# A linear-attention and feed-forward kernel: batch 0's stages in a new order, norms' small values in PSUM, batch 1's attention out in plain float32, dummy matmuls in PE's waits

## The chip, the cores and the metric

One Trainium2 chip, and of it one core. The metric is the device time of one execution in microseconds (us), lower is better. "Time" without more is the median over several runs; a profile shows one execution. The engines are PE (matrix multiplies), DVE (vector), ACT (scalar functions), POOL (GpSimd) and SP, which here only issues DMAs.

## The reference

Linear attention without a softmax over 8 batches of 8 heads (576 tokens, 64 values per head), an RMS norm of each head's output, and a feed-forward block with SiLU over the 4608 tokens:

```python
kv = np.einsum('bhsd,bhse->bhde', k, v)
out = np.einsum('bhsd,bhde->bhse', q, kv)
rms = np.sqrt(np.mean(out * out, axis=-1, keepdims=True) + 1e-06)
x = (out / rms * g_norm)          # transposed to 4608 tokens x 512
h = x @ w_in                      # 512 -> 2048
g = h * (1.0 / (1.0 + np.exp(-h)))
return g @ w_out                  # 2048 -> 512
```

## The kernel before

**Feed-forward.** The 4608 tokens are 9 tiles (t) of 512. Each tile takes 16 steps (f), one for each 128 of the 2048 inner values. A step makes `products` (h of the step: 12 matmuls of 128x512, from the four 128-rows c of x), `gate` (SiLU on ACT twice, and their difference), and `project` of the step two before (12 matmuls into four banks `acc`, one per 128 tokens). There are 144 steps, and PE is given their matmuls in the order of the code.

**Split operands.** A float32 value is kept as two float32r parts, a high one and the rest: `xh` and `xl` for x, `gh` and `gl` for the gate, `w[:, 0]` and `w[:, 1]` for weights. A product takes three matmuls: high by rest, rest by high, high by high. Weights arrive as 64-bit words and are converted block by block, wi0 to wi15 and wo0 to wo15, all during tile 0: `magnitude` (ACT `Abs`, then a clamp on POOL), `bits` (three DVE operations that build the float32 number, through a PSUM tile `conv`), `split_block` (ACT casts the high part, POOL subtracts it for the rest). Step f of tile 0 works on the bits of block wi f+2 and wo f, and splits those of the step before.

**Attention.** A batch is 4 pairs of heads. `mm_kv` makes a pair's two 64x64 kv (20 instructions on PE), ACT copies them to `kvm`, `mm_out` multiplies q by it in two halves of 288 tokens, ACT squares and copies, DVE sums the squares (`sum_sq`). When all 4 pairs are summed, `rsqrt` turns 72 sums per partition into inverse roots by a bit trick and three Newton steps on DVE; before that it adds the two heads' sums across partitions, with four copies of 32 partitions (L397). `spread`, `scale` and `to_tile` then write x. For batches 1 to 7 all of this stands among the feed-forward steps of the tile before: `plan(b, g)` puts each stage into `first_jobs`, `mid_jobs`, `last_jobs` or `chains` of a step, where `mid` stands between products and project. q, kv and kvm are split there (`qh`, `ql`, `kh`, `kl`).

**The start.** Batch 0 has no feed-forward work to stand among. `FirstPair` does its first 512 tokens in plain float32, with tokens on partitions: `make_kv`, `copy_kv`, `make_out` (four matmuls), `square` (ACT), `norm` (`token_norm`: reduce, add eps, inverse root on ACT, one Newton step, multiply to `on`), `make_x` (four transposes on PE), `to_tile`. `Rest` does the last 64 tokens of all four pairs. wi0, wi1 and wi2 are converted in between, the products of steps 0 and 1 are made one c at a time as x comes (`warm`), and `keep_warm` runs matmuls of the identity whose result nobody reads, six at the very start.

What sets the order: every engine runs its instructions in the order of the code, and waits only for the semaphores of what it reads or overwrites. DMAs go through SP's queue, in the order of the list `ORDER` (p is a pair of batch 0, b one of batch 1, g is g_norm).

Of the kernel before, what the change touches and what calls it, by code (L numbers as in the profile page):

```python
# [24 lines left out]
    wi0 p0 g p1 p2 wi1 p3 wi2 wo0 wi3 wo1 wi4 wo2 b0 wi5 wo3 b1 wi6 wo4 wi7 wo5 b2  # L25
# [5 lines left out]
def linear_attention_rms_silu_ffn(  # L31
# [48 lines left out]
    gcol = const.tile([P, 1], F32, name="gcol")  # L80

# [25 lines left out]
    def magnitude(kind, f):  # L107

        full = full_tile(kind, f)
        nc.scalar.activation(out=full, in_=low_high(kind, f)[1].bitcast(F32), func=AF.Abs)  # L110
        nc.gpsimd.tensor_scalar(  # L111
            out=full, in0=full, scalar1=LARGEST, scalar2=SMALLEST, op0=ALU.min, op1=ALU.max
        )

    def bits(kind, f):
# [3 lines left out]

        low, high = low_high(kind, f)  # L120
        first = []
        full = fulls.get((kind, f))
        early = full is None
        if early:
            full = full_tile(kind, f)
            first = [
                lambda: nc.vector.tensor_scalar(
                    out=b, in0=high, scalar1=0x7FFFFFFF, scalar2=None, op0=ALU.bitwise_and
                ),
                lambda: nc.vector.tensor_scalar(  # L130
                    out=full, in0=full, scalar1=SMALLEST, scalar2=LARGEST, op0=ALU.max, op1=ALU.min
                ),
            ]
        b = full.bitcast(I32)
        mids = [b] if early else []
# [6 lines left out]
        return first + [  # L142
# [44 lines left out]
    def newton(y, u, m):  # L187
        return [
            lambda: nc.vector.scalar_tensor_tensor(out=u, in0=y, scalar=-0.5, in1=y, op0=ALU.mult, op1=ALU.mult),
            lambda: nc.vector.tensor_tensor(out=u, in0=u, in1=m, op=ALU.mult),  # L190
            lambda: nc.vector.scalar_tensor_tensor(out=y, in0=u, scalar=1.5, in1=y, op0=ALU.add, op1=ALU.mult),
        ]

    class Pair:


        def __init__(self, b, c):
            self.b, self.c = b, c
            self.kvm = kvm[c if b == 0 else c % 2]
# [11 lines left out]
        def mm_kv(self, kv=None):  # L211
            kv = at_bank() if kv is None else kv
            self.kv = [kv[h * D:(h + 1) * D, 0:D] for h in range(2)]
# [12 lines left out]
        def split_kv(self):  # L226
            self.copy_kv()
            self.kh = kvp.tile([P, P], F32R, name="kh")
# [4 lines left out]
        def split_q(self):  # L233
            self.qh = tmp.tile([P, S], F32R, name="qh", tag="tmp")
# [8 lines left out]
        def mm_out(self, half):  # L243

            self.w = w = slice(half * HS, (half + 1) * HS)
            self.ps = ps = at_bank()[:, :HS]
            nc.tensor.matmul(out=ps, lhsT=self.kh, rhs=self.ql[:, w], start=True, stop=False)  # L247
# [39 lines left out]
    class FirstPair(Pair):  # L287
# [4 lines left out]
        def __init__(self, c):  # L292
            super().__init__(0, c)
            self.ps = at_bank("other") if c == 0 else None

        def make_kv(self):
            self.mm_kv(h_bank())

        def make_out(self):
            self.ps = self.ps or acc_bank()  # L300
# [8 lines left out]
        def norm(self):  # L309
            self.o = tmp.tile([P, S], F32, name="on", tag="tmp")[:, :512]  # L310
            return token_norm(self.o, self.ps, self.sq)
# [12 lines left out]
    class Rest:  # L324
# [13 lines left out]
        def norm(self):  # L338
            self.on = tmp.tile([P, S], F32, name="on", tag="tmp")[:, :256]
            return token_norm(self.on, self.o, self.sq)  # L340
# [16 lines left out]
    def token_norm(o, ps, sq):  # L357

        n = o.shape[1] // D
        m, u, y = (small.tile([P, 8], F32, name=name)[:, :n] for name in ("m0", "u0", "y0"))  # L360
        by_head = [t.rearrange("p (j d) -> p j d", d=D) for t in (o, ps, sq)]
        return [
            lambda: nc.vector.tensor_reduce(out=m, in_=by_head[2], axis=AX.X, op=ALU.add),
            lambda: nc.vector.tensor_scalar(
                out=m, in0=m, scalar1=1.0, scalar2=D * EPS, op0=ALU.mult, op1=ALU.add
            ),
            lambda: nc.scalar.activation(out=y, in_=m, func=AF.Abs_reciprocal_sqrt),
        ] + newton(y, u, m) + [
# [136 lines left out]
    with tc.manual_schedule():  # L505
# [78 lines left out]
        for f in range(WARM):  # L584
            products(warm[f], 0, f, 2)
# [96 lines left out]
```

## Time and profile before

| | |
|---|---|
| median of 3 runs | 897.2 us (897.12 to 897.44) |
| the profiled execution | 895.82 us, of which span 894.0 us |
| mean granted PE clock | 0.988 |
| PE busy | 869.1 us (97%) |
| DVE, ACT, POOL busy | 320.1, 302.7, 175.8 us |
| PE busy from 0 to 36 us | 26.56 us |
| PE busy from 36 to 46 us | 5.00 us |
| PE busy from 46 to 136 us | 82.63 us |

How to read it: the span is the time from the first to the last instruction of one execution, and the rest of its time lies around it. PE's busy time counts a matmul as long as its record says, so a matmul at half the clock counts twice as much. Steps of tile 0 can be told in the timeline by the `products` of line 428 with the tile `hp`: those of step 2 begin at 41.82 us, those of step 15 at 130.49 us.

### The profile page before, as it was taken

The numbers are of one execution on the slowest core, as the hardware profiler recorded it, in microseconds if no ns is written. First come the engines' busy times: TensorE is split into PE (matmuls) and PEld (weight loads), VectorE is DVE, ScalarE is ACT, GpSimd is POOL, SyncE is SP. The second block draws the span as 40 slices with busy tenths as digits, with TensorE's granted clock in tenths as the row PEclk, the third lists the DMA queues.
The fourth block names the chain that finished last, engine by engine and source line by source line (L and its number), as shares of the span: only waits on it lengthen the run. The fifth ranks groups of instructions, "written<-read, shape, count | busy, mean of one in ns | idle before, by whom it ended". The sixth has DMA issues, their size and how long they took to land.

```text
span 894.0 us, 10971 instructions
## 1 busy us (share of the span) xinstructions
PE 869.1 (97%) x4382; PEld 712.4 (80%) x4382; DVE 320.1 (36%) x588; ACT 302.7 (34%) x675; POOL 175.8 (20%) x172
## 2 busy tenths in 40 slices
PE   7689989999999999999999999999999999999998
PEld 5468868888888888888888888888888888888887
DVE  3788894224132423232333223231523141111111
ACT  3457734332243224322433234322432231112112
POOL 1388964101121002101210112010210020000000
PEclk9799999999999999999999999999999999999999
DMA  9538302310042003200311013100300010001001
GB/s 334 233 135 338 111 1 75 93 40 0 1 138 69 1 1 127 80 1 0 114 54 40 1 63 105 41 1 1 127 1 0 1 48 1 0 1 48 1 1 47
DMA packets 23971, 55.23 MB, mean 62 GB/s; under 512 B 2800, under 2 KB 3056, under 8 KB 23920
## 3 DMA queue, kind: packets, MB, share of 16 engines
q1 hardware_dynamic: 23920, 54.54, 17.7%
q8 instruction: 34, 0.56, 0.3%
q14 instruction: 17, 0.14, 0.0%
HBM read 45.09 MB, written 9.44 MB: 61 GB/s over the span
## 4 chain that ended last, share of the span: by engine, by line
PE 86%; DVE 5%; POOL 4%; issue 2%; ACT 1%; DMA 1%; SPq 0%; DVEq 0%; POOLq 0%; ACTq 0%
PE hp L428 40%; PE acc L458 40%; PE at L217 2%; POOL wi L158 1%; POOL full L111 1%; POOL gl L439 1%; PE at L248 1%; PE at L249 1%; PE at L247 1%; PE at L458 1%; DVE m L397 1%; DVE full L149 1%; DMA early_wi<-in_v 1%; PE hp L217 1%; DVE full L130 0%
## 5 line engine op out<-in xcount | busy, mean ns | idle before, releaser
L428 PE MATMUL hp<-xh,wi 128*128 128x512 f32 x1144 | 356.4, 393 | 1.9 <-POOL wi L158 1.9
L458 PE MATMUL acc<-wo,gh 128*128 128x512 f32 (+1 forms) x1152 | 355.2, 390 | 0.0
L439 DVE TENSOR_TENSOR gl<-gf,gh 128x512 fp32r<-128x512 f32 x128 | 88.7, 693 | 499.8 <-ACT gf L438 499.8
L428 PEld LDWEIGHTS hp<-xh,wi 128*128 128x128 f32 x1144 | 217.0, 190 | 45.8 <-POOL wi L158 2.5
L458 PEld LDWEIGHTS acc<-wo,gh 128*128 128x128 f32 x1152 | 214.9, 188 | 44.0
L428 PE MATMUL hp<-xl,wi 128*128 128x512 f32 x572 | 228.5, 400 | 3.5 <-ACT wi L157 3.5
L437 ACT ACTIVATE gh<-hp 128x512 fp32r<-128x512 f32 x143 | 85.5, 598 | 416.6 <-PE hp L428 416.4
L458 PE MATMUL acc<-wo,gl 128*128 128x512 f32 x576 | 222.5, 386 | 0.0
L428 PEld LDWEIGHTS hp<-xl,wi 128*128 128x128 f32 x572 | 108.5, 190 | 26.7 <-ACT wi L157 3.9
L458 PEld LDWEIGHTS acc<-wo,gl 128*128 128x128 f32 x576 | 108.2, 188 | 23.8
L283 POOL TENSOR_TENSOR xl<-o,xh 128x448 fp32r<-128x448 f32 (+7 forms) x56 | 53.2, 952 | 343.4 <-ACT xh L282 343.4
L438 ACT ACTIVATE gf<-hp 128x512 f32<-128x512 f32 x143 | 84.7, 592 | 0.0
L237 POOL TENSOR_TENSOR ql<-q,qh 128x576 fp32r<-128x576 f32 x28 | 40.1, 1432 | 176.3 <-ACT qh L236 172.2
L253 ACT ACTIVATE sq<-at 128x288 f32<-128x288 f32 x56 | 23.2, 414 | 39.6 <-PE at L249 39.6
L274 DVE SCALAR_TENSOR_TENSOR o<-o,gcol,yT 128x448 f32<-128x448 f32 (+7 forms) x56 | 33.8, 604 | 2.0
L224 ACT COPY kvm<-at 64x64 f32<-64x64 f32 x56 | 11.6, 207 | 58.5 <-PE at L217 58.2
L217 PEld LDWEIGHTS at<-v,k 128*64 128x64 f32 (+1 forms) x560 | 20.8, 136 | 13.3 <-issue 9.7
L217 PE MATMUL at<-v,k 128*64 128x64 f32 (+1 forms) x560 | 26.5, 231 | 1.2 <-ACT o L254 1.2
L282 ACT CAST xh<-o 128x448 fp32r<-128x448 f32 (+7 forms) x56 | 24.8, 442 | 5.0 <-DVE o L274 5.0
L267 DVE STREAM_TRANSPOSE yT<-y 128x448 f32<-128x448 f32 (+7 forms) x56 | 26.4, 471 | 0.0
L158 POOL TENSOR_TENSOR wi<-full,wi 128x512 fp32r<-128x512 f32 x16 | 20.8, 1301 | 20.3 <-ACT wi L157 20.3
L254 ACT COPY o<-at 128x288 f32<-128x288 f32 x56 | 22.7, 406 | 4.2 <-POOL xl L283 4.2
(98 smaller groups left out, 481.0 us busy)
## 6 DMA issues: line engine op xcount, KB each, us to landing
out<-ob SPq DMA_DIRECT2D x35, 256.0 KB, 2.3
wi<-in_moe_w_in SPq DMA_DIRECT2D x16, 512.0 KB, 8.1
wo<-in_moe_w_out SPq DMA_DIRECT2D x16, 512.0 KB, 9.2
k<-in_k SPq DMA_DIRECT2D x28, 288.0 KB, 2.9
v<-in_v SPq DMA_DIRECT2D x28, 288.0 KB, 3.2
q<-in_q SPq DMA_DIRECT2D x28, 288.0 KB, 2.9
early_wo<-in_k SPq DMA_DIRECT2D x2, 288.0 KB, 4.8
early_wi<-in_v SPq DMA_DIRECT2D x2, 288.0 KB, 5.1
```

The lines of the kernel that those rows point to most:

```text
L158: nc.gpsimd.tensor_tensor(out=w[:, 1, :], in0=full, in1=w[:, 0, :].bitcast(F32), op=ALU.subtract)
L217: nc.tensor.matmul(out=self.kv[h], lhsT=self.k[rows, c, :], rhs=self.v[rows, c, :], start=(r == 0), stop=(r == 4))
L237: nc.gpsimd.tensor_tensor(out=self.ql, in0=self.q, in1=self.qh.bitcast(F32), op=ALU.subtract)
L267: nc.vector.transpose(out=self.yT.rearrange("p (j a) -> p j a", a=32), in_=y[:, a // 32:e // 32].unsqueeze(2).to_broadcast([P, (e - a) // ...
L274: nc.vector.scalar_tensor_tensor(out=self.o[:, a:e], in0=self.o[:, a:e], scalar=gcol, in1=self.yT, op0=ALU.mult, op1=ALU.mult)
L282: nc.scalar.copy(out=th[:, self.c, w], in_=self.o[:, a:e])
L283: nc.gpsimd.tensor_tensor(out=tl[:, self.c, w], in0=self.o[:, a:e], in1=th[:, self.c, w].bitcast(F32), op=ALU.subtract)
L428: nc.tensor.matmul(out=hp[:, :TN], lhsT=w[:, a, fs], rhs=x[:, c, :], start=(c == 0 and i == 0), stop=(c == NP - 1 and i == 2),)
L437: nc.scalar.activation(out=gh, in_=hp[:, :TN], func=AF.Silu)
L438: nc.scalar.activation(out=gf, in_=hp[:, :TN], func=AF.Silu)
L439: (nc.gpsimd if t == 0 else nc.vector).tensor_tensor(out=gl, in0=gf, in1=gh.bitcast(F32), op=ALU.subtract)
L458: nc.tensor.matmul(out=bank, lhsT=g[:, ns], rhs=w[:, a, cs], start=(f == 0 and i == 0), stop=(f == NF - 1 and i == 2))
```

## The change

- **Order of the start.** Loads: pair 0's k, v and q now come before wi0, and wi1 before pairs 1 to 3. The stages of the four pairs, the conversions of wi0, wi1, wi2 and wo0 and the products of steps 0 and 1 are written out one call after another in a new order; the conversions go through `magnitude` and `conv`, and x of pairs 0, 2 and 3 (before: 2 and 3) is made the shorter way (`fast`). The products of step 2 now precede the transposes of `Rest`.
- **Dummies.** 41 identity matmuls in place of 6, at 10 places of the start.
- **Small values in PSUM.** `token_norm` keeps its sums and intermediate values in a PSUM bank (`stats`), and eps goes into the bias of the activation and into the Newton step. In `rsqrt` two float32 matmuls (L408, L409: `ones` by a row of D*EPS, and `both`, which adds partition blocks of 32 in twos, by the sums) put m into PSUM, in place of four copies and an addition; this holds for all batches from 1 on.
- **Batch 1.** `plain = b < 2`: q, kv and kvm are not split, and a half of out is one float32 matmul. Its stages stand closer together (`stage`, by thirds of a step), begin at step 3 instead of 2, and its `rsqrt` stands in step 11 instead of 12.

```diff
-    wi0 p0 g p1 p2 wi1 p3 wi2 wo0 wi3 wo1 wi4 wo2 b0 wi5 wo3 b1 wi6 wo4 wi7 wo5 b2
+    p0 wi0 g wi1 p1 p2 p3 wi2 wo0 wi3 wo1 wi4 wo2 b0 wi5 wo3 b1 wi6 wo4 wi7 wo5 b2
...
+    both = const.tile([P, P], F32, name="both")
+    nc.gpsimd.tensor_copy(out=both, in_=ident)
+    for i in range(4):
+        nc.gpsimd.tensor_copy(
+            out=both[32 * i:32 * i + 32, 32 * (i ^ 1):32 * (i ^ 1) + 32], in_=ident[32 * i:32 * i + 32, 32 * i:32 * i + 32]
+        )
+    ones = const.tile([1, 2 * P], F32, name="ones")
...
-    def newton(y, u, m):
+    def newton(y, u, m, eps=0.0):
+
         return [
-            lambda: nc.vector.scalar_tensor_tensor(out=u, in0=y, scalar=-0.5, in1=y, op0=ALU.mult, op1=ALU.mult),
-            lambda: nc.vector.tensor_tensor(out=u, in0=u, in1=m, op=ALU.mult),
+            lambda: nc.vector.scalar_tensor_tensor(out=u, in0=m, scalar=eps, in1=y, op0=ALU.add, op1=ALU.mult),
+            lambda: nc.vector.scalar_tensor_tensor(out=u, in0=u, scalar=-0.5, in1=y, op0=ALU.mult, op1=ALU.mult),
...
+            self.plain = b < 2
...
+            if self.plain:
+                nc.tensor.matmul(out=ps, lhsT=self.kvm, rhs=self.q[:, w], start=True, stop=True)
+                return
             nc.tensor.matmul(out=ps, lhsT=self.kh, rhs=self.ql[:, w], start=True, stop=False)
...
-        m, u = (small.tile(sums.shape, F32, name=name) for name in ("m", "u"))
-        calls = [
-            lambda i=i: nc.vector.tensor_copy(
-                out=m[32 * i:32 * i + 32], in_=sums[32 * (i ^ 1):32 * (i ^ 1) + 32]
-            )
-            for i in range(4)
-        ]
...
+        n = NP * (S // 32)
+        bank = at_bank()
+        m, u = bank[:, 0:n], bank[:, n:2 * n]
+        sums, y = (t.rearrange("p c j -> p (c j)") for t in (sums, y))
+        nc.tensor.matmul(out=m, lhsT=ones[:, :P], rhs=ones[:, P:P + n], start=True, stop=False)
+        nc.tensor.matmul(out=m, lhsT=both, rhs=sums, start=False, stop=True)
...
+            if b == 1:
+                k = 3 * g + 1 + 4 * p.c
+                stage(k, p.mm_kv)
+                stage(k + 1, p.split_kv)
+                stage(k + 2, p.begin_out, half[0])
+                stage(k + 3, half[1])
+                stage(k + 5, *[begin] * (p.c == 0), sums)
+                continue
...
-        second = plan(1, 2)
+        second = plan(1, 3)
...
-        keep_warm(6)
...
+        keep_warm(10)
         p0.make_kv()
+        keep_warm(2)
         p0.copy_kv()
+        magnitude("wi", 0, True)
+        w("wi0", 1)
+        p0.make_out()
+        keep_warm(8)
...
-        at(last_jobs, 1, rest.make_x, lambda: moves.extend(rest.to_tile()), lambda: moves.pop(0)())
+        at(mid_jobs, 2, rest.make_x, lambda: moves.extend(rest.to_tile()), lambda: moves.pop(0)())
```

What the new order comes to, engine by engine (numbers behind a name tell one buffer from another; `early_wi` and `early_wo` are batch 0's k, v and q, which lie in places of later weights).

PE, the start, before: dummies, then the pairs' kv (L217), out (L303) and transposes (L316).

```order
L526 MATMUL hp<-ident 128x128 x6
L217 MATMUL hp<-early_wi_114,early_wo_113 64x64 x10
L303 MATMUL at<-kvm_91,early_wo_115 128x128 x4
L217 MATMUL hp<-early_wo_122,early_wi_121 64x64 x10
L303 MATMUL acc<-kvm_92,early_wi_123 128x128 x4
L217 MATMUL hp<-early_wi_128,early_wo_127 64x64 x10
L316 MATMUL at<-ident,on 128x128 x4
L303 MATMUL acc<-kvm_93,early_wo_129 128x128 x4
```

PE, the same place after (L222 is kv, L314 out, L327 a transpose, L542 a dummy):

```order
L542 MATMUL hp<-ident 128x128 x10
L222 MATMUL hp<-early_wi_122,early_wo_121 64x64 x10
L542 MATMUL hp<-ident 128x128 x2
L314 MATMUL acc<-kvm_91,early_wo_123 128x128 x4
L542 MATMUL hp<-ident 128x128 x8
L222 MATMUL hp<-early_wo_134,early_wi_133 64x64 x10
L542 MATMUL hp<-ident 128x128 x2
L327 MATMUL acc<-ident,on 128x128 x4
L314 MATMUL acc<-kvm_92,early_wi_135 128x128 x4
L542 MATMUL hp<-ident 128x128
L222 MATMUL hp<-early_wi_140,early_wo_139 64x64 x10
```

The real work keeps its order but for pair 0's transposes, which now come ahead of pair 1's out, and dummies fill the places between.

DVE, tile 0, before: the chain of batch 1's norms in step 12, one for one among the conversions of wi14 (213) and wo12 (215); the names `m`, `u`, `y` are in SBUF, `conv` is in PSUM.

```order
L143 TENSOR_SCALAR conv<-full 128x512
L397 COPY m<-sums 32x72
L146 SCALAR_TENSOR_TENSOR conv<-wi_213,conv 128x512
L397 COPY m<-sums 32x72
L149 SCALAR_TENSOR_TENSOR full<-wi_213,conv 128x512
L397 COPY m<-sums 32x72
L143 TENSOR_SCALAR conv<-full 128x512
L397 COPY m<-sums 32x72
L146 SCALAR_TENSOR_TENSOR conv<-wo_215,conv 128x512
L402 SCALAR_TENSOR_TENSOR m<-m,sums 128x72
```

DVE, after, in step 11, among the conversions of wi13 (219) and wo11 (221); `at` is the PSUM bank with m and u:

```order
L146 TENSOR_SCALAR conv<-full 128x512
L410 TENSOR_SCALAR y<-at 128x72
L149 SCALAR_TENSOR_TENSOR conv<-wi_219,conv 128x512
L193 SCALAR_TENSOR_TENSOR at<-at,y 128x72
L152 SCALAR_TENSOR_TENSOR full<-wi_219,conv 128x512
L194 SCALAR_TENSOR_TENSOR at<-at,y 128x72
L146 TENSOR_SCALAR conv<-full 128x512
L195 SCALAR_TENSOR_TENSOR y<-at,y 128x72
```

The copies and the addition are gone, the chain has ten operations instead of fifteen, and it starts a step earlier.

PE, the end of the start, before: last products of steps 0 and 1, transposes of `Rest` (L345), products of step 2 (wi_425).

```order
L428 MATMUL acc<-xl_311,wi_380 128x512
L428 MATMUL acc<-xh_310,wi_380 128x512 x2
L345 MATMUL at<-ident,on 128x128 x2
L428 MATMUL hp<-xl_311,wi_425 128x512
L428 MATMUL hp<-xh_310,wi_425 128x512 x2
```

PE, the same place after (wi_460 is step 2's block, L356 the transposes of `Rest`, L462 the first project):

```order
L432 MATMUL acc<-xl_318,wi_432 128x512
L432 MATMUL acc<-xh_317,wi_432 128x512 x2
L432 MATMUL hp<-xl_318,wi_460 128x512
L432 MATMUL hp<-xh_317,wi_460 128x512 x2
L356 MATMUL at<-ident,on 128x128 x2
L462 MATMUL acc<-wo_488,gh 128x512 x2
```

All twelve products of step 2 (two rows of them are shown) now stand ahead of the transposes of `Rest`.

More of the change, by code (lines that the diff above doesn't have):

```diff
@@ L581, in linear_attention_rms_silu_ffn @@
[L581 to L582 removed]
+        n(p2, 4)
+        x(p1, 2)
+        magnitude("wi", 2)
+        n(p3, 2)
+        p2.make_x()
+        warm_products(0, 0)
+        keep_warm(6, kv_bank)
+        w("wi1", 1)
+        n(p3, 4)
+        split("wi", 1)
+        x(p2, 2, True)
+        w("wi2", 1)
+        p3.make_x()
+        magnitude("wo", 0)
+        warm_products(1, 0)
+        keep_warm(1, kv_bank)
+        x(p3, 2, True)
+        warm_products(0, 1)
+        warm_products(1, 1)
@@ L583, in linear_attention_rms_silu_ffn @@
+        w("wi2", 2)
         split("wi", 2)
-        for f in range(WARM):
-            products(warm[f], 0, f, 2)
+        warm_products(2, 0, 1)
+        rest = Rest()
         rest.make_out()
         rest.square()
+        magnitude("wi", 3)
+        w("wo0", 1)
         rest_norm = rest.norm()
-        wo0 = bits("wo", 0)
-        run(wo0[:3])
-        run(rest_norm[:3])
+        run(rest_norm[:2])
+        w("wo0", 2)
         table(AF.Silu)
-        run(wo0[3:])
         split("wo", 0)
-        at(chains, 0, lambda: rest_norm[3:])
+        run(rest_norm[2:])
```

185 lines of the change are left out of this document (99 added, 86 removed).

## The prediction

> **What bounds the kernel now.** I read the page's engine lines and slices first:
>
> ```profile
> span 894.0 us, 10971 instructions
> PE 869.1 (97%) x4382; PEld 712.4 (80%) x4382; DVE 320.1 (36%) x588; ACT 302.7 (34%) x675; POOL 175.8 (20%) x172
> PEclk9799999999999999999999999999999999999999
> ```
>
> PE has work in 97% of the span. So a faster helper engine is worth nothing by itself; the change can only take out time in which PE waits, or runs at half clock, and pays for each matmul it adds. Busy time by stretches says where those are (columns: stretch, its length, busy PE, PEld, DVE, ACT, POOL, granted clock, DMA):
>
> ```profile
> 16.40:19.80 3.40, 1.65 (x14) 1.29 (x14) 0.94 (x2) 1.84 (x6) 1.26 (x1) 0.99 1.02 405
> 19.80:30.00 10.20, 7.79 (x42) 6.38 (x43) 7.50 (x16) 4.21 (x9) 2.54 (x2) 0.50 1.04 402
> 36.50:41.50 5.00, 0.01 (x1) 0.02 (x1) 4.69 (x12) 3.07 (x7) 1.38 (x2) 0.87 0.00 0
> 41.50:47.00 5.50, 5.49 (x14) 4.44 (x15) 5.36 (x6) 3.79 (x8) 5.50 (x5) 0.50 0.00 1
> 47.00:126.80 79.80, 76.76 (x405) 61.88 (x403) 68.35 (x101) 49.19 (x105) 66.13 (x65) 1.00 0.44 164
> 126.80:131.90 5.10, 0.77 (x3) 0.24 (x2) 4.82 (x8) 1.44 (x3) 3.96 (x3) 1.00 0.02 3
> 131.90:136.00 4.10, 4.10 (x11) 3.23 (x12) 4.00 (x7) 3.19 (x6) 3.23 (x3) 0.58 0.00 2
> 136.00:801.00 665.00, 665.00 (x3341) 545.00 (x3341) 200.42 (x397) 211.25 (x488) 89.22 (x82) 1.00 0.13 41
> ```
>
> From 136 us on PE never stops, so everything is decided before. There are two places: the first 47 us (batch 0's stages, 5 us without PE at 36.5, half clock twice), and 126.8 to 136. PE's waits name them:
>
> ```profile
> PE at L345 <- DVE on L369: 5.0, 1, 5.0
> PE acc L303 <- ACT kvm L224: 4.1, 3, 1.8
> PE hp L428 <- ACT wi L157: 3.5, 1, 3.5
> ```
>
> **Term A, the start up to step 2's products.** Before, these start at 41.82. Durations, from the timeline and the chain (start, length, ...) and from the groups by form of 0 to 46 us (mean ns before the bar's idle part):
>
> ```profile
> 1.92 2.93 PE L526 MATMUL hp<-ident 128*128 128x128 f32 x12 [1.92 <-POOL ident masks.py:199]
> 14.65 1.53 PE L217 MATMUL hp<-early_wi,early_wo 128*64 128x64 f32 x20
> 16.11 0.72 PE L316 MATMUL at<-ident,on 128*128 128x128 f32 x4
> 18.59 1.16 PE L303 MATMUL acc<-kvm,early_wo 128*128 128x128 f32 x8 [1.75 <-ACT kvm L224]
> 24.05 2.08 PE L303 MATMUL acc<-kvm,early_wi 128*128 128x128 f32 x8 [1.80 <-ACT kvm L224]
> 41.82 0.78 PE L428 MATMUL hp<-xl,wi 128*128 128x512 f32 x1
> 49.91 0.95 PE L217 MATMUL at<-v,k 128*64 128x64 f32 x20
> 158.20 2.94 PE hp L428 x12
> L307 ACT ACTIVATE sq<-acc 128x512 f32<-128x512 f32 x3 | 1.8, 597 | 3.8 <-PE acc L303 3.8
> L224 ACT COPY kvm<-hp 64x64 f32<-64x64 f32 x8 | 1.6, 206 | 6.8 <-PE hp L217 6.8
> L363 DVE TENSOR_REDUCE m<-sq 128x8 f32<-128x512 f32 x4 | 2.7, 682 | 5.3 <-ACT sq L307 5.3
> L369 DVE TENSOR_TENSOR on<-acc,y 128x512 f32<-128x512 f32 x3 | 2.1, 692 | 0.3
> L146 DVE SCALAR_TENSOR_TENSOR full<-wo,full 128x512 int32<-128x512 int32 x1 | 0.7, 685 | 0.0
> L367 ACT ACTIVATE y<-m 128x8 f32<-128x8 f32 x4 | 0.8, 209 | 2.7 <-DVE m L364 2.7
> L191 DVE SCALAR_TENSOR_TENSOR y<-u,y 128x8 f32<-128x8 f32 x4 | 0.7, 166 | 0.1
> ```
>
> The clock doubles every PE price: kv 1.53 against 0.95, out 2.08 against 1.16. (Until 16 us the clock column reads full, but the 1.53 at 14.65 is a half-clock length: here the lengths are to be trusted.) A dummy costs 2.93/6 = 0.49 at half clock, 0.25 at full. In the new order PE begins at 2.0, as before, with ten dummies: to 6.9. If they bring the full clock, pair 0's kv ends at 7.9, its copies (2 x 0.21) at 8.4, out at 9.6, square 10.3, reduce 11.0, the weight operation put between 11.7, three small operations 12.3, on 13.0. PE meanwhile does eight dummies (2.0), pair 1's kv and two dummies: 13.05. From there PE's own list is the longest: three out (3.5), two kv (1.9), four times four transposes (2.9), 19 dummies (4.8), 24 products (5.9, twice the row of 12), the rest's out (0.5, an estimate: fewer columns than half an out): 19.5, so step 2 starts at 32.5. I went through ACT and DVE pair by pair with the same rows: on 3 is there at 25.2 for a transpose at 25.6, and the last x some 2 us before its use. The loads: pair 0's now come ahead of wi0, so earlier than before; wi1 (512 KB) now passes p1 and p2 on SP's queue, 1.3 us at the 400 GB/s of the rows above, which kv 1 at 11.6 leaves room for within 0.3. POOL's copies for `both` lie before its first subtraction. The m + eps operation goes into ACT's bias, one of 0.17 less per pair. **A = 32.5 - 41.8 = -9.3.** Bounds: 2 us earlier, 3.5 later (0.05 to 0.1 more at each of some 35 hand-overs, a clock that comes one stretch of 3.4 us late).
>
> **Term B.** Step 2's products take 47.0 - 41.8 = 5.2 at half clock, 2.9 at full: **-2.3**, with the rest's transposes now behind them.
>
> **Term C, stalls from 47 to 126.8:** 79.80 - 76.76 = 3.0 before. New ones come at step 2: after it ACT still has the table load, wo0's upper half, one magnitude and two SiLUs, and POOL gl, so the third project matmul waits some 1.8, and step 3's low half (POOL, after two gl) 1.3. POOL does five such things per step (two splits, two magnitudes, gl), and ql is gone for batch 1 (so are qh and kh on ACT and kl on DVE, which lay beside PE and count as nothing):
>
> ```profile
> 46.00:136.00 90.00, 74.31 (x72) 0.98 0.39 145
> L237 POOL TENSOR_TENSOR ql<-q,qh 128x576 fp32r<-128x576 f32 x4 | 5.8, 1456 | 4.2 <-ACT qh L236 4.2
> ```
>
> That leaves 68.5 us of POOL work for a stretch of some 84, 82% as before: PE stays the bound. **C = +0.3**, bounds -3 (nothing waits) and +4 (each step of a conversion late once). SP's loads of b2 and b3 wait for kv and now for out in place of POOL's ql; those come 9 us earlier too.
>
> **Term D, the end of tile 0.** The chain of batch 1's norms stands among the conversions of wi14 and wo12 on DVE:
>
> ```profile
> 110.82 1.30 POOL L158 TENSOR_TENSOR wi<-full,wi 128x512 fp32r<-128x512 f32 x1
> 111.03 3.54 DVE L397 COPY m<-sums 32x72 f32<-32x72 f32 x1
> 112.07 1.30 POOL L158 TENSOR_TENSOR wo<-full,wo 128x512 fp32r<-128x512 f32 x1
> 113.33 1.20 POOL L111 TENSOR_SCALAR full<-full 128x512 f32<-128x512 f32 x2
> 116.63 0.19 DVE L397 COPY m<-sums 32x72 f32<-32x72 f32 x1
> 130.49 0.50 PE L428 MATMUL hp<-xl,wi 128*128 128x512 f32 x1 [3.48 <-ACT wi L157]
> ```
>
> The same copy of 72 elements takes 0.19, or 3.54 for as long as POOL is busy from 110.82 to 114.53. DVE falls behind, wi15 is converted last, PE waits 5.10 - 0.77 = 4.3 and then runs 4.1 us at 0.58, of which 1.6 are lost. After, the four copies and the sum are two matmuls, the ten operations left have at most one SBUF input, and the chain stands a step earlier: 10 x 0.25 + 6 x 0.69 = 6.6 us of DVE in that step, then 1.35 + 4.1 in the next two, against 5.5 of PE: 1 us behind, with a step's slack. **D = -5.9**, bounds 0 and -5.9.
>
> **Terms E and F, work added on PE.** Batch 1's out: three matmuls of 0.13 per half before; plain float32 has no row of 288 columns. Out at full clock spaces its 8 instructions by (1.16 - 0.29)/7 = 0.124 per 128 columns, so 0.56 for 288: +0.17 eight times, **E = +1.3** (to 2.1 if 1.16 is scaled whole). The sums' two matmuls of 72 columns are four such instructions, 0.28 to 0.5 us; I take 0.35, nearer to scaling by columns, in seven batches: **F = +2.4**. All of it is on PE's path; after 136 us it is the only term.
>
> Sum: -9.3 - 2.3 + 0.3 - 5.9 + 1.3 + 2.4 = **-13.5**. The profiled execution took 895.8 (span 894.0 and 1.8 around it), so 882.3; the median of the runs, 897.2, lies 1.4 above it: **883.7**.
>
> **A rule against it.** The row of 16.4 to 19.8 has PE busy 1.65 of 3.4, longest gap 1.75, and 10.2 us at half clock follow. C's two gaps lie in one such stretch, and a stretch of dense PE at half clock costs 1.6 (D's row). The Trainium skill, TensorE: Matmul & The Clock Gate, "Why this matters for your kernels", wants no gap over about 3 us and would charge nothing for these; by its rule the sum stays -13.5, by the row it is -11.9. I go by the sum without it and keep 1.6 in the range. The page's "free-running" window of 3.4 us also means that the first full clock can come later in one execution than in another, which this one trace cannot show.
>
> **Rivals.**
> 1. Slower: the dummies don't bring the full clock, and stand ahead of the real work. Then PE's whole start, some 25 us at full clock (10.3 of it 41 dummies), takes 50: step 2 at 52.3, A = +10.5, B = 0, and the sum +8.6: 905.8. It decides once some 14 us of those 25 run at half clock. Against it: between 13 and 16.4 PE worked without a gap, and the 0.72 and 1.16 rows followed at full clock. 4%.
> 2. POOL sets tile 0's pace, or DVE's small operations stay slow in PSUM (the change doesn't do what it says there): the end of tile 0 still stalls, D = 0, 889.6. For it: POOL is busy 82%; against: conversions with one PSUM operand keep 0.69 beside POOL. 13%.
> 3. The start is bound by ACT, DVE and loads, so full clock buys half of it: A + B = -7, 888.3. 10%.
> 4. All stalls go, C = -3, A two better: 878.4. 8%.
>
> **How the numbers follow.** My forecast (881 to 887 with its own bounds) has 65%. 0.2% (1.8 us) is about what a measurement of this kernel can tell. The range 877.5 to 890.5 holds rivals 2 to 4 and leaves out rival 1 and some 15% of tails. Faster 0.95: all but rival 1 and a sum of bad bounds; same 0.01; slower 0.04.
>
> **What would show it.** Right: kv and out of pairs 1 to 3 at 0.95 and 1.16, step 2's products near 32 and in 2.9 us, no DVE operation of 72 elements over 0.4, no PE wait over 1 us between 60 us and the end, L408 and L409 under 0.5 us per batch. Wrong: clock 0.50 in the first 30 us after 9, PE waiting for POOL's splits in steps 5 to 15, or a wait of the sums' matmul for DVE in later batches, which would come seven times.

## The result: slower by 0.9%, and the profile after

The changed kernel takes 904.57 us (904.15 to 904.71), the kernel before 897.16 beside it on the same chip: ratio 1.0087, 95% interval 1.0066 to 1.0107. The forecast was 883.7, in a range of 877.5 to 890.5. (A fourth run of the changed kernel took 2233 us, for which nothing here shows a reason: the ratio leaves it out, and without it the median is 904.43.) The profiled execution took 904.43 us with a span of 902.7. Of its page, the header and the engines' line:

```profile
span 902.7 us, 11085 instructions
PE 878.6 (97%) x4472; PEld 717.3 (79%) x4472; DVE 300.5 (33%) x535; ACT 301.8 (33%) x671; POOL 210.0 (23%) x180
```

POOL is busy 210.0 us, where it was 175.8, although four `ql` of 1.46 us are gone. Busy time by stretches, columns as in the prediction:

```profile
0.00:36.50 36.50, 32.43 (x258) 27.88 (x258) 21.25 (x46) 19.27 (x41) 18.45 (x30) 1.00 0.94 347
36.50:47.00 10.50, 7.32 (x20) 5.47 (x21) 6.24 (x9) 6.80 (x13) 10.50 (x8) 0.74 0.01 2
47.00:126.80 79.80, 70.16 (x357) 53.83 (x355) 55.83 (x88) 41.46 (x87) 79.80 (x55) 0.99 0.44 163
126.80:136.00 9.20, 6.59 (x27) 5.10 (x28) 8.21 (x8) 4.16 (x8) 9.20 (x8) 1.00 0.00 1
```

The first row is near what was hoped for: PE is busy 32.43 of 36.50 us, where it was 27.06. (The clock column alone doesn't prove the full clock there, as the prediction found; the lengths do: pair 1's kv takes 0.95 us and its out 1.06.) From 36.5 to 136 us POOL, the fifth busy figure, has no free moment: 10.50 of 10.50, 79.80 of 79.80, 9.20 of 9.20. PE's waits name it:

```profile
PE hp L432 <- POOL wi L161: 11.0, 7, 2.8
PE acc L462 <- POOL gl L443: 2.4, 1, 2.4
PE hp L432 <- POOL xl L295: 1.5, 1, 1.5
```

What POOL does there is told by its groups from 47 to 126.8 us, here the two largest of the changed kernel:

```profile
L127 POOL TENSOR_SCALAR full<-full 128x512 f32<-128x512 f32 x22 | 41.7, 1909 | 0.0
L443 POOL TENSOR_TENSOR gl<-gf,gh 128x512 fp32r<-128x512 f32 x11 | 14.1, 1283 | 0.0
```

and the clamp in the same stretch of the kernel before:

```profile
L111 POOL TENSOR_SCALAR full<-full 128x512 f32<-128x512 f32 x23 | 13.8, 618 | 0.0
```

The clamp of a block's magnitudes took 0.62 us and takes 1.91, on the same 128x512 elements. The diff has the likely reason in a line that neither the list of changes nor the prediction mentions: the two bounds and operations stand in the other order.

```diff
-        nc.gpsimd.tensor_scalar(
-            out=full, in0=full, scalar1=LARGEST, scalar2=SMALLEST, op0=ALU.min, op1=ALU.max
+        (nc.vector if on_vector else nc.gpsimd).tensor_scalar(
+            out=full, in0=full, scalar1=SMALLEST, scalar2=LARGEST, op0=ALU.max, op1=ALU.min
```

The other order isn't new: six early conversions of the kernel before have it, but on DVE, where a clamp takes 0.43 us (L130). The change makes one function of the two, so that POOL does 31 clamps instead of 26, all in DVE's order.

Theory 1 of the experiments: this order costs POOL 31 x 1.29 = 40 us, it becomes the bound of tile 0, and all else is as forecast. Its rivals: the new order of the stages itself overloads POOL or DVE, or the 1.91 come from what runs beside the clamps.

### The profile page after: what moved, and what is told of

Read it like the earlier page. It is cut to its first block, busy times and chain, and to the rows that moved or that the text cites. A ratio compares the mean times of both kernels' runs of the same rounds, so it can differ in the third digit from the quotient of the medians.

```text
span 902.7 us, 11085 instructions
## 1 busy us (share of the span) xinstructions
PE 878.6 (97%) x4472; PEld 717.3 (79%) x4472; DVE 300.5 (33%) x535; ACT 301.8 (33%) x671; POOL 210.0 (23%) x180
## 4 chain that ended last, share of the span: by engine, by line
PE 84%; POOL 0%; ACT 0%; issue 0%; ACTq 0%
PE hp L432 39%; PE acc L462 39%; PE at L222 2%; PE at L260 1%; PE at L261 1%; PE at L259 1%; PE at L462 1%; PE at L409 0%; PE at L408 0%; POOL xl L295 0%; ACT ob L467 0%; ACTq L467 0%
## 5 line engine op out<-in xcount | busy, mean ns | idle before, releaser
L432 PE MATMUL hp<-xh,wi 128*128 128x512 f32 x1144 | 355.3, 392 | 11.0 <-POOL wi L161 11.0
L462 PE MATMUL acc<-wo,gh 128*128 128x512 f32 (+1 forms) x1152 | 357.4, 392 | 0.1
L432 PEld LDWEIGHTS hp<-xh,wi 128*128 128x128 f32 x1144 | 215.0, 188 | 56.6 <-POOL wi L161 13.9
L462 PEld LDWEIGHTS acc<-wo,gh 128*128 128x128 f32 x1152 | 215.5, 189 | 44.8 <-POOL wo L161 0.3
L432 PE MATMUL hp<-xl,wi 128*128 128x512 f32 x572 | 228.2, 399 | 1.5 <-POOL xl L295 1.5
L462 PE MATMUL acc<-wo,gl 128*128 128x512 f32 x576 | 223.3, 388 | 2.4 <-POOL gl L443 2.4
L462 PEld LDWEIGHTS acc<-wo,gl 128*128 128x128 f32 x576 | 108.6, 189 | 26.6 <-POOL gl L443 2.8
L432 PEld LDWEIGHTS hp<-xl,wi 128*128 128x128 f32 x572 | 107.7, 188 | 24.5 <-POOL xl L295 1.9
L246 POOL TENSOR_TENSOR ql<-q,qh 128x576 fp32r<-128x576 f32 x24 | 34.2, 1425 | 173.2 <-ACT qh L245 168.2
L127 POOL TENSOR_SCALAR full<-full 128x512 f32<-128x512 f32 x31 | 58.9, 1910 | 0.9 <-ACT full L126 0.9
L286 DVE SCALAR_TENSOR_TENSOR o<-o,gcol,yT 128x448 f32<-128x448 f32 (+7 forms) x56 | 39.0, 696 | 2.0
L146 DVE TENSOR_SCALAR conv<-full 128x512 int32<-128x512 int32 x32 | 22.2, 694 | 30.7 <-POOL full L127 29.4
L222 PEld LDWEIGHTS at<-v,k 128*64 128x64 f32 (+1 forms) x560 | 20.8, 136 | 14.3 <-issue 8.9
L222 PE MATMUL at<-v,k 128*64 128x64 f32 (+1 forms) x560 | 26.5, 231 | 1.9 <-ACT o L266 1.9
```

Source lines behind the costliest of these rows:

```text
L127: (nc.vector if on_vector else nc.gpsimd).tensor_scalar(out=full, in0=full, scalar1=SMALLEST, scalar2=LARGEST, op0=ALU.max, op1=ALU.min)
L222: nc.tensor.matmul(out=self.kv[h], lhsT=self.k[rows, c, :], rhs=self.v[rows, c, :], start=(r == 0), stop=(r == 4))
L246: nc.gpsimd.tensor_tensor(out=self.ql, in0=self.q, in1=self.qh.bitcast(F32), op=ALU.subtract)
L286: nc.vector.scalar_tensor_tensor(out=self.o[:, a:e], in0=self.o[:, a:e], scalar=gcol, in1=self.yT, op0=ALU.mult, op1=ALU.mult)
L432: nc.tensor.matmul(out=hp[:, :TN], lhsT=w[:, a, fs], rhs=x[:, c, :], start=(c == 0 and i == 0), stop=(c == NP - 1 and i == 2),)
L462: nc.tensor.matmul(out=bank, lhsT=g[:, ns], rhs=w[:, a, cs], start=(f == 0 and i == 0), stop=(f == NF - 1 and i == 2))
```

## Experiments

Unless said otherwise a difference between two of them is between medians. e1 to e4, e5 to e8, e9 to e12, and e13 with e14 are four groups: each group has its own chip and its own runs of the kernel before. Between groups the ratios to the kernel before are compared too.

### e1: the clamp's order alone put back

```diff
-            out=full, in0=full, scalar1=SMALLEST, scalar2=LARGEST, op0=ALU.max, op1=ALU.min
+            out=full, in0=full, scalar1=LARGEST, scalar2=SMALLEST, op0=ALU.min, op1=ALU.max
```

> The changed kernel, but POOL's clamp of the magnitudes (31 of 128x512) is min with LARGEST first, then max with SMALLEST, as in the kernel before; everything else stays. Theory 1 (the order of the two operations costs POOL 1.91 us in place of 0.62, 31 times, 40 us, so that POOL is the bound of tile 0: it is busy 79.8 of the 79.8 us from 47 to 126.8): each clamp is back at about 0.62, POOL has slack in tile 0, no wait of PE for POOL over 1 us after 60 us, and the time is what the prediction's other terms give, 880 to 886 us, ratio to before 0.981 to 0.988. Rival (the new order itself makes POOL or DVE the bound of tile 0, by the five more clamps and by contention; the clamp's order only shows it): POOL stays busy over 95% of tile 0, PE keeps waiting for POOL, 893 us or more.

883.82 us (883.13 to 883.92), ratio 0.9856 (0.9838 to 0.9875): 20.7 us under the changed kernel by one pair of swapped arguments. The clamp's row, and the stretches of tile 0:

```profile
L127 POOL TENSOR_SCALAR full<-full x31: 604/611/627, 16.9 to 114.5; 128x512 f32<-128x512 f32 x31
```

```profile
36.50:47.00 10.50, 9.61 (x58) 7.33 (x57) 8.80 (x13) 7.74 (x18) 10.50 (x12) 1.00 0.18 59
47.00:126.80 79.80, 78.16 (x388) 62.48 (x388) 60.15 (x95) 45.25 (x94) 64.29 (x61) 1.00 0.42 156
126.80:136.00 9.20, 9.20 (x58) 7.68 (x59) 2.75 (x6) 4.45 (x11) 1.89 (x2) 1.00 0.23 84
```

POOL has 15.5 us of room from 47 to 126.8, PE loses 1.6 there instead of 9.6, and from 69 us on it waits for nothing. Theory 1 holds; the rival is out.

### e2: the kernel before with the swapped order

```diff
-            out=full, in0=full, scalar1=LARGEST, scalar2=SMALLEST, op0=ALU.min, op1=ALU.max
+            out=full, in0=full, scalar1=SMALLEST, scalar2=LARGEST, op0=ALU.max, op1=ALU.min
```

> The kernel before, but POOL's clamp (26 of 128x512) is max with SMALLEST first, then min with LARGEST. Theory 1: each takes 1.9 us in place of 0.62, +1.29 x 26 = 33 us of POOL; from 47 to 126.8 POOL had 66.1 of 79.8 us and would need some 95, so tile 0 is bound by POOL: 907 to 920 us, ratio 1.011 to 1.026. Rival (the 1.9 us come from what stands beside the clamps in the changed kernel, such as DVE's conversions through PSUM, and not from their order): the clamps stay near 0.62 and the time at 896 to 898.

916.95 us, ratio 1.0224 (1.0199 to 1.0249), within the 907 to 920. The clamps (x26) take 1.91 to 2.29 us, and POOL is full:

```profile
47.00:126.80 79.80, 66.56 (x336) 52.15 (x335) 51.76 (x77) 43.86 (x95) 79.80 (x54) 0.94 0.44 163
```

So the line does the same harm without the rest of the change.

### e3: the price of the operation by itself

Eleven kinds of `tensor_scalar` in place on a scratch tile, one per step, in the kernel before at times when POOL idles; each has its own line, as in

```diff
+        lambda: nc.gpsimd.tensor_scalar(scalar1=LARGEST, scalar2=SMALLEST, op0=ALU.min, op1=ALU.max, **io),
+        lambda: nc.gpsimd.tensor_scalar(scalar1=SMALLEST, scalar2=LARGEST, op0=ALU.max, op1=ALU.min, **io),
```

> The kernel before, with one operation on a scratch tile of 128x512 in each of the first steps of tiles 2, 4 and 6, where POOL is busy about a seventh of the time; eleven kinds, on lines of their own: nine on POOL (min then max, max then min, max alone, min alone, multiply then add, max then max, min then min, and min then max and max then min with the bounds 4 and 1) and the two clamps on DVE. It prices the operation by itself. Theory 1: on POOL max then min takes about 1.9 us and min then max about 0.6 also with nothing beside them, whatever the bounds; on DVE both take 0.43. Rival A (contention in tile 0 makes the 1.9): both take 0.6. Rival B (it is the small bound 2^-15 as the first number, not the order): max then min is slow with LARGEST and SMALLEST and fast with 1 and 4, and max alone with SMALLEST is slow. The time stays within 0.3% of before, since none of it is on PE's path.

Its groups by form, in the order min-max (L85), max-min (L86), max alone, min alone, multiply-add (L89), max-max, min-min, min-max with 4 and 1 (L94), max-min with 1 and 4 (L95), and max-min on DVE (L93):

```profile
L85 POOL TENSOR_SCALAR scr<-scr 128x512 f32<-128x512 f32 x3 | 1.8, 615 | 4.6 <-ACT scr L647 4.5
...
L86 POOL TENSOR_SCALAR scr<-scr 128x512 f32<-128x512 f32 x3 | 5.8, 1917 | 0.0
...
L87 POOL TENSOR_SCALAR scr<-scr 128x512 f32<-128x512 f32 x3 | 4.5, 1490 | 0.0
...
L88 POOL TENSOR_SCALAR scr<-scr 128x512 f32<-128x512 f32 x3 | 4.5, 1492 | 0.0
...
L89 POOL TENSOR_SCALAR scr<-scr 128x512 f32<-128x512 f32 x3 | 2.3, 772 | 0.3
...
L90 POOL TENSOR_SCALAR scr<-scr 128x512 f32<-128x512 f32 x3 | 5.8, 1937 | 0.0
...
L91 POOL TENSOR_SCALAR scr<-scr 128x512 f32<-128x512 f32 x3 | 5.8, 1932 | 0.2
...
L94 POOL TENSOR_SCALAR scr<-scr 128x512 f32<-128x512 f32 x3 | 1.8, 616 | 24.6 <-DVE scr L93 24.6
...
L95 POOL TENSOR_SCALAR scr<-scr 128x512 f32<-128x512 f32 x3 | 5.8, 1924 | 0.2
...
L93 DVE TENSOR_SCALAR scr<-scr 128x512 f32<-128x512 f32 x3 | 1.3, 419 | 0.0
```

The order decides, alone and whatever the bounds; contention and the small bound are both out. Max-min isn't the odd one out: of the seven kinds on POOL only min-max and multiply-add are fast, and a max or a min alone takes 1.49, more than twice the pair min-max. On DVE max-min takes 0.42. The time, 895.37 in its one run, stays.

### e4: without the added dummies

```diff
-            for _ in range(n):
+            for _ in range(6 if n == 10 else 0):
```

> The same as e1_clamp_order_back, but of the 41 dummy matmuls only the first group stays, with six in place of ten, so that PE waits again where they stood. Theory (the prediction's terms A and B: the dummies bring the full clock to the first 34 us): the start falls back to half clock in at least two stretches, kv and out of pairs 1 to 3 are at 1.5 and 2.1 us again, step 2's products start 4 us or more later, at 36 or after, and the time is 4 to 10 us over e1. Rival (the new order alone fills PE, the dummies only add 5 to 10 us of PE): step 2's products start as in e1 or earlier, and the time is within 1 us of e1 or below it.

Of the 41 dummies the first six stay, as many as the kernel before has; 35 go. 884.96 us (884.00 to 886.02) against e1's 883.82: 1.1 us. The clock is what the theory said, half until 21 us; two kv and an out of the timeline:

```profile
4.92 1.53 PE L222 MATMUL hp<-early_wi,early_wo 128*64 128x64 f32 x20
15.72 1.53 PE L222 MATMUL hp<-early_wi,early_wo 128*64 128x64 f32 x20
21.84 1.16 PE L314 MATMUL acc<-kvm,early_wi 128*128 128x128 f32 x8
```

Yet step 2's products start at 32.57, 2.4 later than in e1 (30.18), not 4 or more, and 9.3 earlier than before. The rival is nearer: the order fills PE's waits, and most of what half clock costs lies in them. The 35 dummies are worth 1.1 us by the medians; by the two profiled executions it is 2.9 (spans 881.3 and 884.2).

### e5: batch 1 split as before

```diff
-            self.plain = b < 2
+            self.plain = b < 1
...
-                stage(k + 1, p.split_kv)
+                stage(k + 1, p.split_kv, p.split_q)
```

> The same as e1_clamp_order_back, but batch 1's out is made from split operands (three matmuls per half, with kh, kl, qh and ql, ql on POOL) as in the kernel before, at the new order's places. Theory (term E: plain float32 costs PE 0.17 us more for each of 8 halves, 1.3 in all, and POOL has room for four ql of 1.46): 1.3 us faster than e1, 882.5. Rival (POOL at 64 of 79.8 us in tile 0 and DVE are so near the bound that ql, kl and the waits for them cost more than PE saves): 884.5 to 888, with a PE wait for POOL ql.

891.38 us, ratio 0.9952 (0.9940 to 0.9965), 7.6 over e1 by the medians and 8.6 by the ratios: the rival, and dearer than it said. Its waits:

```profile
PE at L259 <- POOL ql L246: 6.4, 3, 4.0
```

The wait of 4.0 is followed by 6.8 us at clock 0.50 (47.02 to 53.84), a part of the price. In the changed kernel plain float32 isn't a small cost on PE but what keeps `ql` out of POOL's queue in tile 0.

### e6 and e7: where the norms' small values lie

e6 makes them in SBUF for batches 1 to 7, e7 in PSUM for batch 1 and in SBUF for the others; the old form of `rsqrt` is in the diff of the change.

```diff
-        at(chains, s + 4, lambda: rsqrt(*norms))
+        at(chains, s + 4, lambda: rsqrt(*norms, b == 1))
```

> The same as e1_clamp_order_back, but the reciprocal roots of batches 1 to 7 are made as before: four copies of 32x72 between partitions and one sum on DVE in SBUF in place of the two matmuls on L408 and L409; the chain still starts a step earlier than in the kernel before. The trace of e1 shows 0.70 us of PE for the two matmuls (92.98 to 93.68), so leaving them out frees 7 x 0.70 = 4.9 us of PE. Theory (term D: it was PSUM that took the small operations off POOL's way; a copy of 72 elements waits up to 3.5 us for POOL): some of the copies take 1 to 3.5 us in tile 0, DVE falls behind and PE waits 2 to 5 us for the last conversions of tile 0; with the 4.9 that comes to 879 to 884. Rival (the earlier chain alone gives D): no wait over 1 us at the end of tile 0, 879 or less.

> The same as e1_clamp_order_back, but the norms' values are in PSUM, with the two matmuls, for batch 1 alone; batches 2 to 7 use the four copies on DVE as before, where POOL is busy about a seventh of the time. Theory (term F: the two matmuls are on PE's path in every batch, 0.70 us each by e1's trace, not 0.35): 6 x 0.70 = 4.2 us faster than e1, 879.6. Rival (0.35 as predicted): 2.1 faster, 881.7. Other rival (the copies come late for the x of later batches): a PE wait for xh or xl once a batch, 884 or more.

890.69 and 888.37 us: ratios 0.9944 (0.9932 to 0.9957) and 0.9917 (0.9903 to 0.9930). Both are slower than e1, by 6.9 and 4.6, where 879 to 884 and 879.6 were expected, and no wait accounts for it. e7's trace has none over 1.1 us behind the start, and PE is busy without a gap from 136 us on; it only does less in the same time. One stretch of 95 us, of e7 and of e1:

```profile
231.00:326.00 95.00, 95.00 (x484) 76.87 (x483) 28.53 (x59) 30.57 (x73) 12.52 (x12) 1.00 0.15 49
```

```profile
231.00:326.00 95.00, 95.00 (x489) 77.57 (x488) 28.55 (x55) 30.62 (x73) 11.92 (x11) 1.00 0.14 45
```

484 matmuls for 489, at clock 1.00 in both. Worked out from the starts of successive matmuls of the two traces between 150 and 840 us: a matmul on gh or gl comes after 229.3 ns in e1 and after 234.2 in e7, one on x after 227.6 and 229.5, and so it is from the first step on, where the two kernels' PE instructions are the same. What differs is that two small tiles of the old `rsqrt` stand ahead of the gate tiles (gh, gf, gl) and move these by 1152 B. So e6 and e7 tell nothing of D and F; e9 to e11 do.

### e8: the slow order for half of the clamps

```diff
+        if kind == "wi":
+            order = dict(scalar1=SMALLEST, scalar2=LARGEST, op0=ALU.max, op1=ALU.min)
```

> The same as e1_clamp_order_back, but the clamp is max then min for the wi blocks (15 on POOL) and min then max for the wo blocks (16): half of the slow clamps. Theory (POOL is bound only beyond a threshold): 15 x 1.29 = 19 us more of POOL; from 47 to 126.8 e1 has 79.8 - 64.3 = 15.5 us of room, so POOL just becomes the bound: 3 to 8 us over e1, 887 to 892, much less than half of the 20.7 us between e1 and the changed kernel. Rival (each slow clamp is waited for once, wherever it stands): half of the 20.7, 894.

888.99 us, ratio 0.9927 (0.9913 to 0.9941), 5.2 over e1 by the medians and 6.4 by the ratios: a quarter or a third of the 20.7 for half of the clamps. POOL is nearly full:

```profile
47.00:126.80 79.80, 77.24 (x379) 60.97 (x378) 64.66 (x96) 45.80 (x97) 77.38 (x64) 1.00 0.44 162
```

### e9, e10 and e11: the gate tiles kept, or moved alone

e9 is e7 and e11 is e6 with the two small tiles in a pool behind the gate tiles; e10 is e1 with an unused tile ahead of them, and no instruction differs:

```diff
+    pad = ctx.enter_context(tc.tile_pool(name="pad", bufs=1))
+    pad.tile([P, 288], F32, name="pad")
     gp = ctx.enter_context(tc.tile_pool(name="gp", bufs=LAG + 1))
```

> The same as e7_psum_batch1_only (norms in PSUM for batch 1 alone), but the two small tiles m and u of the old form lie behind the gate tiles gh, gf and gl in SBUF, so that these keep the addresses that they have in e1. In e7 they lay 1152 B further up, and its trace shows 484 matmuls per 95 us where e1 has 490, from the first step of tile 0 on, with the same matmuls in the same order. Theory (the address of the gate tiles alone slowed every matmul of e7): the count per 95 us is back at 490 or over, and without the two matmuls in six batches the time is 4.2 us under e1, 879.6. Rival (the copies on DVE in the later batches slow PE): still 484, 888.

> The same as e1_clamp_order_back, with an unused tile of 1152 B ahead of the gate tiles in SBUF; no instruction differs. Theory (addresses): the matmuls that read gh and gl come every 233 ns and not 229, the others every 229 and not 227, 484 per 95 us, and the time is some 9 us over e1, 893. Rival (something else in e6 and e7): 883.8, as e1.

> The same as e6_norms_in_sbuf (all norms on DVE in SBUF), with m and u behind the gate tiles, whose addresses are those of e1. e6 showed two waits of 0.9 us at the end of tile 0 that e1 does not have. Theory (term D: the order and the earlier chain give most of D, PSUM only the last 2 us): 4.9 us of PE saved and 2 lost, 881 or a little under; that is 1 to 2 us over e9. Rival (PSUM is needed for all of D): 884 or more.

e9 takes 878.59 us (ratio 0.9814, 0.9801 to 0.9827), e10 893.59 (0.9980, 0.9971 to 0.9989), e11 881.41 (0.9845, 0.9832 to 0.9859). The stretch from above, of e9 and of e10:

```profile
231.00:326.00 95.00, 95.00 (x489) 77.78 (x488) 29.98 (x61) 30.94 (x74) 12.69 (x12) 1.00 0.15 49
```

```profile
231.00:326.00 95.00, 95.00 (x484) 76.64 (x484) 27.70 (x55) 29.69 (x72) 12.53 (x12) 1.00 0.15 49
```

An unused tile of 1152 B costs 9.8 us by the medians, 11.1 by the ratios: shown. With the place kept, leaving the two matmuls out of six batches gains 5.2 us by the medians and 3.8 by the ratios; 6 x 0.70 = 4.2 was expected. e11, without PSUM in batch 1 as well, is 2.8 over e9; its waits:

```profile
PE hp L437 <- POOL wi L162: 2.4, 3, 0.9
...
PE hp L437 <- POOL xl L296: 1.0, 1, 1.0
```

and its first copy of 72 elements takes 1.30 beside a POOL operation, not 3.54.

### e12: three places for the gate tiles in one kernel

```diff
+    for i, n in enumerate((0, 16, 32)):
+        if n:
+            ctx.enter_context(tc.tile_pool(name=f"pad{i}", bufs=1)).tile([P, n], F32, name=f"pad{i}")
+        gps.append(ctx.enter_context(tc.tile_pool(name=f"gp{i}", bufs=1)))
```

> The same as e1_clamp_order_back, but the three pairs of gate tiles lie in three pools with 64 and 128 B between them: the first at the address of e1, the second 64 B and the third 192 B further up, counted modulo 512. So the interval of the matmuls of each third of the steps shows what these addresses do. Theory (the place modulo 256 against the weight tiles sets it): steps on the first pair show 229 ns; the other two differ from it and from each other by some ns. Rival (it is a matter of 1 KB or more): all three thirds alike, at 229 or at 233.

885.42 us, 1.6 over e1 by the medians and 3.2 by the ratios. The mean interval of the matmuls on gh and gl, from their starts in the trace, by steps in threes: 229.3 ns on the first pair (e1's place), 226.7 on the second (64 B up), 233.1 on the third (192 B up).

### e13 and e14: 64 B up, in the fastest version and in the kernel before

```diff
+    pad.tile([P, 16], F32, name="pad")
     gp = ctx.enter_context(tc.tile_pool(name="gp", bufs=LAG + 1))
```

> The same as e9_psum_batch1_layout_kept, with an unused tile of 64 B ahead of the gate tiles, so that all three pairs lie 64 B further up: where the middle third of e12 lay, whose 512-column matmuls on gh and gl came every 226.7 ns in place of 229.3. Theory (the place of the gate tiles sets it): 1728 such matmuls x 2.6 ns = 4.5 us under e9, 874.1. Rival (in e12 the three pairs lay otherwise to each other, and that gave the middle third its 226.7): as e9, 878.6.

> The kernel before, with the same unused tile of 64 B ahead of the gate tiles. They then lie to the weight tiles, modulo 256 B, as in e13. Theory: the loop of the kernel before, whose matmuls show the same 226, 229 and 232 ns as e1, goes to 226.7 too, and the kernel gains the same 4.5 us, 890.7 by the median of before of the last set, 895.1: then none of the difference between before and after lies in the place of these tiles. Rival (the places of the other tiles, which differ between before and after, decide): within 1 us of before, or slower; then a part of the change's result is a matter of place.

e13 takes 874.87 us (874.70 to 875.59), ratio 0.9767 (0.9753 to 0.9782), 3.7 under e9 by the medians and 4.2 by the ratios. It beats both kernels and does 492 matmuls in the stretch:

```profile
231.00:326.00 95.00, 95.00 (x492) 78.19 (x491) 29.97 (x61) 31.34 (x74) 12.71 (x12) 1.00 0.16 50
```

e14 takes 893.28 against 896.06, ratio 0.9970 (0.9960 to 0.9981); its interval goes from 229.3 to 226.7 ns as e13's does, and from tile 1's first product to the end its trace takes 751.8 us for 755.2. The gain of 1.7 to 3.6 us is less than the 4.5 expected (its start, with half clocks and waits, differs from run to run), but place had no share in the miss: before and after stood at the same 229.3.

## Why the prediction was wrong

The step that failed is **term C**, with the conversions' price in it: "POOL does five such things per step (two splits, two magnitudes, gl)... 68.5 us of POOL work for a stretch of some 84, 82% as before: PE stays the bound." The 68.5 are the 74.31 of the kernel before less `ql`, so the magnitudes went in at their old price (1.20 us for two in D's rows), though their order of operations was changed; two take 3.8. Then POOL's full step is 2 x 1.91 + 2 x 1.28 + 1.28 = 7.7 us against 5.5 of PE (with the old order 5.1); in the trace POOL starts a `gl` every 7.5 us for most of tile 0. With the old order the 82% was right: 64.29 of 79.80, 81%, in e1. C came to +0.3 within -3 and +4; rival 2, "POOL sets tile 0's pace", had the mechanism, but with D = 0 for its price, 889.6. The prediction's own sign of being wrong, PE waiting for POOL's splits in steps 5 to 15, is what came: six of the seven waits for `wi` lie between 97 and 136 us.

The damage in the changed kernel against e1: tile 1's first product (the 193rd matmul of L432) starts at 140.62 us in its trace and at 121.14 in e1's, 19.5 later, and a wait of 1.5 for `xl` comes behind it:

```profile
140.62 0.39 PE L432 MATMUL hp<-xl,wi 128*128 128x512 f32 x1
```

```profile
121.14 0.39 PE L432 MATMUL hp<-xl,wi 128*128 128x512 f32 x1
```

With the slow line out, e1's profiled execution took 883.13 where the sum gave 882.3, and its median is 883.82 for 883.7. Not all of that is right for the right reasons; the terms, by e1:

- **A**, -9.3 by forecast: step 2's products start at 30.18, so -11.6 (31.49 in the changed kernel). That is 0.3 beyond the bound of 2 us earlier. The list of PE's work added the rows' lengths, but the next group starts before the last matmul of a group ends (pair 1's out, 1.06 long at 13.33, is followed at 14.22): the three outs take 2.8 us for 3.5, the sixteen transposes 1.6 for 2.9. The reason is half wrong: full clock came as forecast (kv 0.95 and out 1.06 from pair 1 on), but e4 shows -9.3 without the 35 dummies, at half clock until 21 us, so most of the gain is the order's, and the dummies add 2.4.
- **B**, -2.3: 30.18 to 32.94 is 2.8 us for 5.2, so -2.4. Right.
- **C**, +0.3, without the slow clamps: the two new waits at steps 2 and 3 are 1.1 and 0.9 us where 1.8 and 1.3 were named, and the stretch of 47 to 126.8 loses 1.6 for 3.0. So 2.0 - 1.4 = +0.6. How +0.3 follows from its own 1.8 + 1.3 - 3.0 the prediction doesn't say.
- **D**, -5.9: all of it: e1's PE has no wait after the one at 68.4 us, and clock 1.00; no DVE operation of 72 elements takes over 0.24 in its tile 0. PSUM isn't what gives most of it: e11 keeps the copies in SBUF, in step 11 instead of 12, and has three waits at the end of tile 0 that e1 has not, 0.55, 0.94 and 0.98, 2.5 us in all, where the kernel before lost 5.9. How the other 3.4 divide between the earlier step and the rest of the change was not tried.
- **E**, +1.3: from the first matmul of a half to the second one behind it are 0.72 us with plain float32 (55.68 to 56.39 in e1, by single matmuls' starts) and 0.64 with split operands (76.08 to 76.72 in the kernel before): 0.08 eight times, +0.6. But the alternative that E was set against, e5, at the new order's places, costs 7.6: that plain float32 frees POOL was costed at nothing, "82% as before".
- **F**, +2.4, mis-sized to less than half. Each pair of matmuls of the sums costs some 0.79, over twice the 0.35 taken and over the bound of 0.5. By the timeline of e1:

```profile
92.75 0.39 PE L462 MATMUL acc<-wo,gl 128*128 128x512 f32 x1
93.07 0.44 PE L408 MATMUL at<-ones 1*128 1x72 f32 x2
93.43 0.44 PE L409 MATMUL at<-sums,both 128*128 128x72 f32 x2
93.68 0.48 PE L432 MATMUL hp<-xl,wi 128*128 128x512 f32 x1
94.00 0.63 PE L432 MATMUL hp<-xh,wi 128*128 128x512 f32 x2
```

From 92.75 to 93.68 are 0.93 us where two neighbours are 0.23 apart: 0.70 more, the figure that the expectations of e6 and e7 use. From 93.68 to 94.00 are 0.32 for 0.23, another 0.09: 0.79, seven times, 5.5. Scaling by columns fails for so short a matmul; each of the four instructions takes some 0.2, close to its weight load (0.18 to 0.19 in the same trace). That the load sets it is not shown. From tile 1's first product to the end, e1 takes 760.2 us, the kernel before 755.2 and e9 755.2: the 5.0 are F, in six batches (6 x 0.79 = 4.7).

In sum e1 gains 17.7 us up to tile 1 (138.82 to 121.14), where 15.6 were forecast, and gives 5.0 back behind it, where 2.1 were: two misses that nearly cancel.

**The rule against it.** In the changed kernel the two gaps that C named did bring the half clock, for the slow clamp made them longer:

```profile
37.82 0.56 PE L462 MATMUL acc<-wo,gl 128*128 128x512 f32 x1 [2.39 <-POOL gl L443]
38.18 1.05 PE L462 MATMUL acc<-wo,gh 128*128 128x512 f32 x2
...
44.05 0.73 PE L432 MATMUL hp<-xh,wi 128*128 128x512 f32 x2 [1.86 <-POOL wi L161]
```

Two matmuls of 512 columns take 1.05 behind the gap for 0.62 at full clock, and the granted clock is 0.50 from 38.12 to 41.53 and from 44.94 to 48.35. The Trainium skill, TensorE: Matmul & The Clock Gate, "Why this matters for your kernels", asks for no gap over about 3 us; here 2.4 sufficed, and the measurement decides. In e1 the same two gaps are 1.09 and 0.89, and the clock holds.

Length alone doesn't decide, though. The longest wait of the changed kernel is followed by clock 1.00:

```profile
128.48 0.74 PE L432 MATMUL hp<-xh,wi 128*128 128x512 f32 x2 [2.81 <-POOL wi L161]
```

The clock changes above lie 3.41 us apart. Counted in stretches of that length, PE is idle for 2.39 us from 34.70 to 38.12 and for 1.86 from 41.53 to 44.94, with half clock behind each; the 2.81 us lie in two such stretches, 1.19 us up to 126.86 and 1.62 behind it. Idle time per stretch fits these better than length, but no sharp limit follows: in the kernel before PE is idle for 1.93 us from 125.52 to 128.94, and the clock stays at 1.00 for the 3.41 us behind it.

**Rivals.** 1 (the dummies stand ahead at half clock): did not occur; that its 905.8 lies next to the measured 904.6 is chance, for the start took 31.49 us to step 2 and not 52.3. 3 (the start bound by ACT, DVE and loads, half the gain): did not occur, A was larger. 4 (all stalls go, 878.4): not at e1; e9 gets there another way.

## What to carry over

Read every changed argument of an instruction as a change of its price: on an engine that runs at 80% of a stretch, one swapped pair of operations that triples a 0.6 us instruction moved the bound and turned -1.4% into +0.9%. Price an engine's work per step against the bound's step before and after (here 5.1 and 7.7 us against 5.5), for the loss begins only where the room is used up: half of the slow clamps cost a third at most. When a variant is slower and no wait says why, count matmuls per stretch at full clock before explaining it by its edit: an added tile may have moved other tiles.

## What the hardware showed that was not expected

- POOL's `tensor_scalar` on 128x512 float32 goes from 0.62 us (min then max) over 0.77 (multiply then add) and 1.49 (max or min alone) to 1.92 to 1.94 (max then min, and either one twice). DVE does both orders in 0.42. The Trainium skill, GPSIMD Engine Reference, "4.1 Engine selection", calls operations of one input roughly line-rate on this engine; the clamps of 1.9 us here, 4.6 times DVE's 0.42, do not bear that out.
- The place of the tiles from which PE loads weights changes the pace of 512-column matmuls at full clock: 226.7, 229.3, 233.1 and 234.2 ns for places 64, 0, 192 and 1152 B above e1's, and the matmuls that read other tiles slow down too (227.6 to 229.6 in e10). Over the kernel that is some 13 us between 64 and 1152 B (3.7 from e9 to e13, 9.8 from e1 to e10, by the medians). Modulo 256 B the distance from the weight blocks of w_out to gh, by the sizes of the tiles between them, is 0, 192, 128 and 64 for these; why that should matter, and whether 256 is the period, was not tried.
